# Attention and token mixing on one core: constants ahead of the queries, a gate behind them, masks behind the scores

## The chip, the core and the metric

The kernel runs on one core of a Trainium2 chip. The core has a matrix engine (TensorE, PE in the profile), a vector engine (VectorE, DVE), a scalar engine (ScalarE, ACT), a general engine (GpSimd, POOL) and a queue engine (SyncE, SP) that issues transfers. Each engine works through its own list of instructions in order and waits on semaphores for the others. The metric is the device time of one execution in microseconds, as the median of several.

## The reference

Three stages follow one another; the first feeds `x` into the second, the second into the third.

```python
# 1  attention: B=2, H=8, S=768, D=64; 32-row blocks, window 16
k_sum = k.reshape(B,H,24,32,D).max(3);  v_sum = v.reshape(B,H,24,32,D).mean(3)
scores_l = where(|i-j| < 16, q @ k.T / 8, -1e9)
scores_s = q @ k_sum.T / 8 + log(32)
a = softmax(concat[scores_l, scores_s]);  x = a @ concat[v, v_sum]
# 2  token mixing: x is (2, 768, 512)
theta = x @ w_theta
y = w_tok_r @ (x*cos(theta)) + w_tok_i @ (x*sin(theta));  u = x + y
x = u + relu(u @ w_ch)
# 3  gated unit
h = gelu(x @ w_in);  u, v = halves(h);  v_n = layernorm(v) * g_ln
out = x + (u * (w_sg @ v_n + b_sg)) @ w_out
```

## The kernel before

**Attention.** The sixteen heads form eight pairs p = 0..7 (four for each batch). One pair has four score groups g = 4p + 2hf + h (hf the half of the rows, h the head). A row block of 64 queries sees a window of 96 keys (WK) and the 24 block summaries (NS), 120 columns (WC) in all. For each half the program has these steps, with the tile names that the trace shows:

- prep_k: `ks` is the block maximum of the keys (DVE); `kv<-k` copies the overlapping windows, `kv<-ks` the summaries behind them.
- prep_v: `vsp` (PE) sums the values by block, `vs` copies the sum out, `kv<-vs` spreads it under each window's values.
- scores: two mask matmuls (bf16, identity times `mask`) write `S` and start the accumulation, then 24 score matmuls add to it. `nb` is the row maximum (DVE), `P` the exponentials (ACT), `PT` the transposed `P` (PE), `Pt` its copy, `O` the product with the values (PE), `ri` and `x` the normalisation (DVE), `X` the transposed result (PE), `xT` its copy.

**Token mixing and the gated unit.** `th` (theta) takes 4 × 3 matmuls of 128x512 for each of twelve row tiles, `xs` being its split input: every fp32 product is three fp32r matmuls, hi·hi, hi·lo and lo·hi. Then come `y` with the weights `w_r` and `w_i`, `ch`, `u`, `sg` and `o`. Weights arrive as raw fp32 and are split by shifts on DVE (`cw_...`, three instructions: shift, shift-and-or, shift-and-or) and copies.

**What sets the order.** Nothing is looped in the final program. A list scheduler (`Plan.play`) assigns each step to an engine and writes each engine's list out, from costs in the text of the kernel, from due times shifted by the table BIAS, from a charge STAY for switching kinds of matmul, from weights LOAD by which an engine is chosen where two or three can do a step (one set before its time 80, another behind it), and from the number of buffers of each kind in HOMES. All loads go through SP's one list, in the order of PLAN["want"]; `theta` in PLAN says where the theta tiles start among the score groups. `warm` at the start runs a row of fills (`wps`), matmuls without use for the result.

Of the kernel before, what the change touches and what calls it, by code (L numbers as in the profile page):

```python
# [24 lines left out]
WK = 96  # L25
# [24 lines left out]
class Plan:  # L50
# [257 lines left out]
    def backlog(self, e, c, ready, ready_t, now):  # L308
# [5 lines left out]
SKIP = {}  # L314
ROUNDS = 1
BIAS = {
    "M": 25, "PT": -2, "S": -1, "abs": 4, "ba_": -5, "blocks": 25, "bs_": 8, "bsg": -24,
    "ch___": -2, "cos": 19, "craw": -6, "g": -5, "gf__": -8, "gm__": -5, "gs__h": -1,
    "gs__l": 15, "id": -18, "ident": 4, "k": 1, "ki": 7, "kk": 13, "kw_": -19, "mask": -10,
    "max": 1, "norm_": 1, "o___": -7, "ob__": 12, "q": -14, "q_": -2, "quarter": -9, "ra": 4,  # L320
    "rb": -4, "rc": -11, "rec_": -3, "sg___": -14, "sin": -6, "small": -4, "sq": 2,
    "st__": 26, "th_": -9, "uT__": 13, "u___": -7, "us__h": 2, "us__l": 8, "v_": -17,
    "v__": 7, "vf_": -4, "vnh_": -4, "vnl_": 21, "vs_": 16, "vsc": -7, "vsg": 1, "vsp": 2,
    "w_ch.": 1, "w_ch.h": -9, "w_ch.hi": -7, "w_ch.lo": 13, "w_i.": -3, "w_i.h": 8,
    "w_i.hi": -12, "w_i.lo": 7, "w_inu.": -9, "w_inu.h": 10, "w_inu.hi": 4, "w_inu.lo": 13,
    "w_inv.": -4, "w_inv.h": 1, "w_inv.hi": 4, "w_inv.lo": -10, "w_out.": 6, "w_out.h": 11,
    "w_out.hi": -14, "w_out.lo": -2, "w_r.": -18, "w_r.hi": -1, "w_r.lo": 9, "w_ri.": 5,
    "w_ri.h": -1, "w_ri.hi": 1, "w_ri.lo": -6, "w_sg.": 8, "w_sg.hi": 24, "w_sg.lo": -7,
    "w_sgs.": 1, "w_sgs.hi": -8, "w_sgs.lo": 8, "w_th.": 1, "w_th.h": -4, "w_th.lo": -2,
    "warm": -21, "warm_end": -10, "xT_": -5, "x__": 8, "xh": 2, "xs__h": 3, "xs__l": -13,  # L330
    "y__": 2, "ys_": -14, "z_": 2, "zeros": -13, "zh_": -6, "zl_": -2,
}
TRACE = 0
STAY = 15.5

LOAD = ({"ACT": 0.71, "DVE": 1.34, "POOL": 0.92}, {"ACT": 0.08, "DVE": 1.79, "POOL": 23.66},
        80.0)

PLAN = {
    "want": [("pair", 0), ("pair", 1), ("th", 0), ("pair", 2), ("pair", 3), ("th", 1), ("pair", 4),
             ("th", 3), ("th", 2), ("pair", 5), ("r", 0), ("i", 0), ("pair", 7), ("pair", 6),
             ("i", 1), ("r", 1)],
    "ahead": 0,
    "theta": [20, 26, 27, 28, 29, 36],
    "filler": 20,
    "prep_v": 0,
    "one": 1,
# [5 lines left out]
def kernel(  # L355
# [131 lines left out]
    def load_pair(p):  # L487
        b, r = divmod(p, NP)
        for hf in range(2):
            plan.at(("q", p, hf), f"kv{p}_0")  # L490
        if p:
            load(f"q{p}", lambda: T(f"kv{p}_0")[:, :S], qT[b, r], [("q", p, 0), ("q", p, 1)])
        else:
            load("q0_0", lambda: T("kv0_0")[:, :S // 2], qT[b, r][:, :S // 2], [("q", p, 0)])
            buf("craw", "t")
            load("craw", lambda: T("craw")[:, :P + 3 * WC], consts, ["craw"])
            load("q0_1", lambda: T("kv0_0")[:, S // 2:S], qT[b, r][:, S // 2:], [("q", p, 1)])
        for j, (t, c, w0, w1) in enumerate(vpart[p]):
# [191 lines left out]
    def scores(p, hf):  # L690

        gs = [4 * p + 2 * hf + h for h in range(2)]
        for g in gs:
            buf(f"S{g}", "ps")
            buf(f"P{g}", "t")
            buf(f"nb{g}", "nb")
            for t in range(3):
                plan.at((f"P{g}", t), f"P{g}")

        def masks(e):  # L700
            for g in gs:
                PE.matmul(T(f"S{g}")[:, :3 * WC], id16[:], mask[:, hf * WC:(hf + 3) * WC], start=True,
                          stop=False, skip_group_check=True)

        def mm(e):
            for t in range(3):
                for ab in range(2):
                    for h, g in enumerate(gs):
                        r0 = slice(64 * h, 64 * h + 64)
                        w = 6 * hf + 2 * t + ab  # L710
                        j, kv, c = window(kpart[p], w, WC)
                        PE.matmul(T(f"S{g}")[64 * ab:64 * ab + 64, t * WC:(t + 1) * WC],
                                  T(f"kv{p}_0")[r0, 64 * w:64 * w + 64], T(kv)[r0, c:c + WC],
                                  start=False, stop=True, skip_group_check=True)

        js = (0,) if hf == 0 else (0, 1)
        ss = [f"S{g}" for g in gs]
        op(f"M{gs[0]}", {"PE": 0.32}, masks, ["id16", "mask", *["mask2"] * hf], ss)
        op(f"S{gs[0]}", {"PE": 0.7}, mm,
           [("q", p, hf), *((x, p, j) for j in js for x in ("k", "ks"))], ss, mode="S")  # L720
        for g in gs:
            ps, pt, nb = f"S{g}", f"P{g}", f"nb{g}"
            op(f"max{g}", {"DVE": 0.51}, lambda e, ps=ps, nb=nb: DVE.tensor_reduce(  # L723
                out=T(nb)[:], in_=T(ps)[:, :3 * WC].rearrange("p (t c) -> p t c", c=WC),
                axis=AX.X, op=ALU.max, negate=True), [ps], [nb])
            for t in range(3):
# [398 lines left out]
    def fill(n, z=None):  # L1125

        for j in range(n):
            PE.matmul(T("wps")[:, :4 * WC], id16[:] if z is None else z[:, :P],
                      mask[:] if z is None else z[:, P:P + 4 * WC], start=True, stop=True)
# [8 lines left out]
        T("zeros")[:, :64 + 2 * WC].bitcast(BF16), 0.0), [], ["zeros"])  # L1138
    op("mask", {"DVE": 0.3}, lambda e: DVE.memset(mask[:], 0.0), [], ["mask"])
    op("small", {"POOL": 0.4}, small, [], ["consts"])  # L1140
    op("warm", {"PE": 4.5}, lambda e: fill(12, T("zeros")[:].bitcast(BF16)), ["zeros"], ["wps"])

    def want_th(c):
        weights(("th", c), [rows(w_theta, c)])
# [214 lines left out]
```

## Time and profile before

| | |
|---|---|
| three timed runs | 397.71, 406.56, 403.67 us, median 403.67 |
| the profiled execution's own time | 399.96 us |
| its span in the trace | 398.2 us (1.8 us lie around it) |
| TensorE busy | 388.1 us, 97% of the span, 2899 matmuls |
| VectorE busy | 282.5 us, 71% |
| ScalarE busy | 199.6 us, 50% |
| GpSimd busy | 49.0 us, 12% |
| TensorE's granted clock, mean | 1.0 of full speed |

The shares are means over the whole span, and the attention part fills roughly the first 80 us of it, beside the theta tiles. The page's slices show GpSimd busy in the first ninety microseconds alone, and the transfers at their highest share up to about 55 us.

### The profile page before, as it was taken

To read this page: it belongs to the slowest core of one execution; us is meant where nothing else is said; L and a number is where in the kernel's file an instruction comes from. 1 tells how busy PE (TensorE), PEld (TensorE's weight loads), DVE (VectorE), ACT (ScalarE), POOL (GpSimd) and SP (SyncE) were. 2 spreads that over 40 slices of the span, in tenths; PEclk is the share of its full clock that TensorE was granted. 3 is DMA by queue.
4 is the path that set the end of the run, shared out by engine and by line. 5 is a ranking of instruction groups with operands and counts; after the bars stand their busy time and mean duration, and the time that the engine had idled before them with its cause. 6 is when DMAs were issued, how large, how long until landed. Compare 5 with 4: busy or idle time off the path is not lost.

```text
span 398.2 us, 7273 instructions
## 1 busy us (share of the span) xinstructions
PE 388.1 (97%) x2899; PEld 324.9 (82%) x2899; DVE 282.5 (71%) x542; ACT 199.6 (50%) x415; POOL 49.0 (12%) x81
## 2 busy tenths in 40 slices
PE   7898999999999999999999999999999999999996
PEld 3666667778888888889999988889888889888986
DVE  3769979999999997689999889483454146315442
ACT  3686878668999943244673516274110035411100
POOL 1567886220000000000000000000000000000000
PEclk9999999999999999999999999999999999999999
DMA  8999995310010011338930032010001101000012
GB/s 229 291 282 297 287 252 200 109 54 2 0 34 20 0 54 53 93 96 299 404 130 0 2 106 105 2 53 2 0 0 43 38 28 40 15 0 0 16 44 102
DMA packets 15970, 37.63 MB, mean 95 GB/s; under 512 B 1984, under 2 KB 4928, under 8 KB 15936
## 3 DMA queue, kind: packets, MB, share of 16 engines
q1 hardware_dynamic: 15936, 37.16, 30.0%
q8 instruction: 23, 0.38, 0.4%
q14 instruction: 11, 0.09, 0.1%
HBM read 34.01 MB, written 3.15 MB: 93 GB/s over the span
## 4 chain that ended last, share of the span: by engine, by line
PE 86%; DMA 9%; DVE 3%; SPq 1%; ACT 1%; issue 0%; DVEq 0%
PE y L444 8%; PE y L443 8%; PE y L445 8%; DMA k<-in_kT_dram 4%; PE sg L445 4%; PE sg L444 4%; PE sg L443 4%; PE th L443 3%; PE ch L445 3%; PE ch L443 3%; PE o L445 3%; PE ch L444 3%; PE o L444 3%; PE o L443 3%; PE u L445 3%; PE u L444 3%
## 5 line engine op out<-in xcount | busy, mean ns | idle before, releaser
L431 ACT ACTIVATE g<-gf 128x512 fp32r<-128x512 f32 (+1 forms) x16 | 8.4, 525 | 59.7 <-DVE gf L1100 59.7
L1097 DVE SCALAR_TENSOR_TENSOR gf<-sg,g_sb,bsg 128x512 f32<-128x512 f32 (+1 forms) x16 | 9.9, 617 | 36.4 <-PE sg L445 36.4
L728 ACT ACTIVATE P<-S,nb 128x120 f32<-128x120 f32 x96 | 27.5, 370 | 8.5 <-DVE nb L723 8.1
L444 PE MATMUL y<-w_ri,zs 128*128 128x256 f32 x96 | 27.1, 282 | 0.0
L443 PE MATMUL y<-w_ri,zs 128*128 128x256 f32 x96 | 27.1, 282 | 0.0
L445 PE MATMUL y<-w_ri,zs 128*128 128x256 f32 x96 | 27.0, 282 | 0.0
L443 PE MATMUL ch<-u,w_ch 128*128 128x512 f32 (+1 forms) x64 | 21.7, 338 | 0.0
L445 PE MATMUL ch<-u,w_ch 128*128 128x512 f32 (+1 forms) x64 | 21.6, 338 | 0.0
L444 PE MATMUL o<-g,w_out 128*128 128x512 f32 (+1 forms) x64 | 21.6, 337 | 0.0
L445 PE MATMUL o<-g,w_out 128*128 128x512 f32 (+1 forms) x64 | 21.6, 337 | 0.0
L444 PE MATMUL ch<-u,w_ch 128*128 128x512 f32 (+1 forms) x64 | 21.6, 337 | 0.0
L443 PE MATMUL o<-g,w_out 128*128 128x512 f32 (+1 forms) x64 | 21.6, 337 | 0.0
L444 PE MATMUL u<-x,w_inu 128*128 128x512 f32 (+1 forms) x64 | 21.5, 336 | 0.0
L443 PE MATMUL u<-x,w_inu 128*128 128x512 f32 (+1 forms) x64 | 21.5, 336 | 0.0
L445 PE MATMUL u<-x,w_inu 128*128 128x512 f32 (+1 forms) x64 | 21.5, 336 | 0.0
L443 PE MATMUL th<-w_th,xs 128*128 128x512 f32 x48 | 20.3, 424 | 0.0
L445 PE MATMUL sg<-w_sg,vn 128*128 128x512 f32 x48 | 19.0, 397 | 0.0
L444 PE MATMUL sg<-w_sg,vn 128*128 128x512 f32 x48 | 19.0, 395 | 0.0
L443 PE MATMUL sg<-w_sg,vn 128*128 128x512 f32 x48 | 18.9, 393 | 0.0
L444 PE MATMUL y<-w_i,zs 128*128 128x512 f32 x48 | 18.8, 392 | 0.0
L445 PE MATMUL th<-w_th,xs 128*128 128x512 f32 x48 | 18.8, 392 | 0.0
L444 PE MATMUL y<-w_r,zs 128*128 128x512 f32 x48 | 18.8, 392 | 0.0
(197 smaller groups left out, 1167.3 us busy)
## 6 DMA issues: line engine op xcount, KB each, us to landing
k<-in_kT_dram SPq DMA_DIRECT2D x8, 384.0 KB, 8.1
w_r<-in_w_rT_dram SPq DMA_DIRECT2D x6, 512.0 KB, 6.4
w_i<-in_w_iT_dram SPq DMA_DIRECT2D x6, 512.0 KB, 4.6
kv<-in_vW_dram SPq DMA_DIRECT2D x8, 341.2 KB, 9.3
kv<-in_qT_dram SPq DMA_DIRECT2D x7, 384.0 KB, 9.5
w_th<-in_w_theta_dram SPq DMA_DIRECT2D x4, 512.0 KB, 7.9
w_ch<-in_w_ch_dram SPq DMA_DIRECT2D x4, 512.0 KB, 4.7
w_inv<-in_w_in_dram SPq DMA_DIRECT2D x4, 512.0 KB, 6.2
```

The lines of the kernel that those rows point to most:

```text
L431: e.activation(dst, src, AF.Copy, scale=scale)
L443: PE.matmul(ps, ah, bh, start=first, stop=False, skip_group_check=True)
L444: PE.matmul(ps, ah, bl, start=False, stop=False, skip_group_check=True)
L445: PE.matmul(ps, al, bh, start=False, stop=last, skip_group_check=True)
L728: ACT.activation(T(pt)[:, t * WC:(t + 1) * WC], T(ps)[:, t * WC:(t + 1) * WC], AF.Exp, bias=T(nb)[:, t:t + 1], scale=1.0),
L1097: lambda e: DVE.scalar_tensor_tensor(out=T(gf)[:, :n], in0=T(ps)[:, :n], scalar=g_sb[:, f:f + 1], in1=T("bsg")[:, o:o + n], op0=ALU.mult, ...
```

## The change

- `craw` (the constants: identity and masks) is loaded second, ahead of both halves of pair 0's queries, and behind these stands a transfer of one element, `gate`, that reads `craw`. It can't be issued before `craw` has landed, and every later load stands behind it in SP's list.
- The mask matmuls stand behind the score matmuls and close the accumulation; they cover the 3 × 96 key columns and no longer the summary columns (288 columns instead of 360). The first score matmuls of each column block start it.
- The row of fills at the start has 9 instead of 12.
- The tables are set anew: BIAS, STAY, LOAD, the load order `want`, the theta starts; buffers of kind c (`cw_`) 3 to 2, of kind r 6 to 7.

By the two programs' lists, VectorE has 508 rows instead of 533, ScalarE 368 instead of 362, GpSimd 103 instead of 86, TensorE 2199 instead of 2203. 24 steps go from VectorE to ScalarE (eight `xT` copies, the copies of five `vsc`, three `Pt` among them) and seven to GpSimd; 16 go from ScalarE to GpSimd (copies of windows and spreads); six go from GpSimd to ScalarE, three to VectorE, and five from ScalarE to VectorE.

```diff
-HOMES = {"w": 31, "t": 7, "c": 3, "r": 6, "x": 4, "ps": 8, "ks": 2, "nb": 4, "ri": 3, "st": 3, "mv": 1, "rs": 1}
+HOMES = {"w": 31, "t": 7, "c": 2, "r": 7, "x": 4, "ps": 8, "ks": 2, "nb": 4, "ri": 3, "st": 3, "mv": 1, "rs": 1}
...
-    "M": 25, "PT": -2, "S": -1, "abs": 4, "ba_": -5, "blocks": 25, "bs_": 8, "bsg": -24,
+    "M": 23, "PT": -9, "PV": -3, "Pt": -2, "S": -8, "X_": 1, "abs": 23, "ba_": -2,
...
-STAY = 15.5
+STAY = 13.5
-
-LOAD = ({"ACT": 0.71, "DVE": 1.34, "POOL": 0.92}, {"ACT": 0.08, "DVE": 1.79, "POOL": 23.66},
+LOAD = ({"ACT": 3.5, "DVE": 7.65, "POOL": 0.67}, {"ACT": 1.31, "DVE": 8.05, "POOL": 98.87},
         80.0)
...
-    "want": [("pair", 0), ("pair", 1), ("th", 0), ("pair", 2), ("pair", 3), ("th", 1), ("pair", 4),
-             ("th", 3), ("th", 2), ("pair", 5), ("r", 0), ("i", 0), ("pair", 7), ("pair", 6),
-             ("i", 1), ("r", 1)],
+    "want": [("pair", 0), ("pair", 1), ("th", 0), ("pair", 2), ("th", 2), ("pair", 3), ("pair", 4), ("th", 1), ("pair", 5), ("th", 3), ("i", 0), ("pair", 7), ("r", 1), ("r", 0),
+             ("i", 1), ("pair", 6)],
     "ahead": 0,
-    "theta": [20, 26, 27, 28, 29, 36],
+    "theta": [23, 23, 24, 29, 29, 34],
...
-            load("q0_0", lambda: T("kv0_0")[:, :S // 2], qT[b, r][:, :S // 2], [("q", p, 0)])
             buf("craw", "t")
             load("craw", lambda: T("craw")[:, :P + 3 * WC], consts, ["craw"])
-            load("q0_1", lambda: T("kv0_0")[:, S // 2:S], qT[b, r][:, S // 2:], [("q", p, 1)])
+            for x in range(2):
+                c0 = x * S // 2
+                load(f"q0_{x}", lambda c0=c0: T("kv0_0")[:, c0:c0 + S // 2],
+                     qT[b, r][:, c0:c0 + S // 2], [("q", p, x)])
+
+            op("gate", {"SP": 0.06}, lambda e: e.dma_start(gate[:], T("craw")[0:1, 0:1]),
+               ["craw"], ["gate"], dma=0.01)
...
-        def masks(e):
-            for g in gs:
-                PE.matmul(T(f"S{g}")[:, :3 * WC], id16[:], mask[:, hf * WC:(hf + 3) * WC], start=True,
-                          stop=False, skip_group_check=True)
-
         def mm(e):
...
-                                  start=False, stop=True, skip_group_check=True)
+                                  start=t == 0, stop=False, skip_group_check=True)
+
+        def masks(e):
+            def keys(x):
+                return x.rearrange("p (t c) -> p t c", c=WC)[:, :, :WK]
+
+            for g in gs:
+                PE.matmul(keys(T(f"S{g}")[:, :3 * WC]), id16[:],
+                          keys(mask[:, hf * WC:(hf + 3) * WC]), start=False, stop=True,
+                          skip_group_check=True)
...
-        op(f"M{gs[0]}", {"PE": 0.32}, masks, ["id16", "mask", *["mask2"] * hf], ss)
         op(f"S{gs[0]}", {"PE": 0.7}, mm,
            [("q", p, hf), *((x, p, j) for j in js for x in ("k", "ks"))], ss, mode="S")
+        op(f"M{gs[0]}", {"PE": 0.28}, masks, ["id16", "mask", *["mask2"] * hf], ss)
...
-    op("warm", {"PE": 4.5}, lambda e: fill(12, T("zeros")[:].bitcast(BF16)), ["zeros"], ["wps"])
+    op("warm", {"PE": 3.6}, lambda e: fill(9, T("zeros")[:].bitcast(BF16)), ["zeros"], ["wps"])
```

Three places of the lists. The number behind a tile's name is the program's own count. First the start of SP's list before: keys of pair 0 (`k0`), its queries in halves (`kv0_0`), the constants, its values (`kv0_2`, `kv0_3`, `kv0_0`), the keys of pair 1.

```order
L472 DMA k0_79<-in_kT_dram 128x768
L472 DMA kv0_0_81<-in_qT_dram 128x384
L472 DMA craw_83<-in_consts_dram 128x488
L472 DMA kv0_0_81<-in_qT_dram 128x384
L472 DMA kv0_2_86<-in_vW_dram 96x520
```

The same place now.

```order
L474 DMA k0_81<-in_kT_dram 128x768
L474 DMA craw_83<-in_consts_dram 128x488
L474 DMA kv0_0_85<-in_qT_dram 128x384 x2
L503 DMA gate_72<-craw_83 1x1
L474 DMA kv0_2_106<-in_vW_dram 96x520
```

The constants moved one place forward, and a transfer that waits for them came between the queries and the values. Next, SP's list ahead of pair 6's keys (`k6`), which are the last keys to come; before:

```order
L472 DMA kv5_0_152<-in_vW_dram 96x130
L472 DMA w_r0_327<-in_w_rT_dram 128x512
L472 DMA w_i0_374<-in_w_iT_dram 128x512
L472 DMA k7_398<-in_kT_dram 128x768
L472 DMA kv7_0_400<-in_qT_dram 128x768
L472 DMA kv7_2_473<-in_vW_dram 96x520
L472 DMA kv7_3_483<-in_vW_dram 96x910
L472 DMA kv7_0_400<-in_vW_dram 96x130
L472 DMA k6_577<-in_kT_dram 128x768
```

And now, from the same place:

```order
L474 DMA kv5_0_166<-in_vW_dram 96x130
L474 DMA w_th3_249<-in_w_theta_dram 128x512
L474 DMA w_i0_326<-in_w_iT_dram 128x512
L474 DMA k7_380<-in_kT_dram 128x768
L474 DMA kv7_0_386<-in_qT_dram 128x768
L474 DMA kv7_2_423<-in_vW_dram 96x520
L474 DMA kv7_3_498<-in_vW_dram 96x910
L474 DMA kv7_0_386<-in_vW_dram 96x130
L474 DMA w_r1_508<-in_w_rT_dram 128x512
L474 DMA w_r0_558<-in_w_rT_dram 128x512
L474 DMA w_i1_595<-in_w_iT_dram 128x512
L474 DMA k6_597<-in_kT_dram 128x768
```

`w_r1` and `w_i1` moved ahead of pair 6's keys; the other weights there were ahead of them before too, so it is two more weight blocks. Last, VectorE's list around pair 6's block maximum `ks6` before:

```order
L723 TENSOR_REDUCE nb19_950<-S19_884 128x3
L614 TENSOR_REDUCE ks6_961<-k6_577 128x24
L786 TENSOR_SCALAR ri4_0_987<-O4_0_952 128x6
L789 RECIPROCAL ri4_0_987<-ri4_0_987 128x6
L783 TENSOR_TENSOR x1_0_993<-O4_0_952,ri4_0_987 128x3x128
L723 TENSOR_REDUCE nb20_1001<-S20_946 128x3
```

VectorE's list around `ks6` now:

```order
L795 TENSOR_TENSOR x1_0_1015<-O4_0_936,ri4_0_1009 128x3x128
L440 COPY vs_71<-vsp5_975 24x130
L621 TENSOR_REDUCE ks6_1026<-k6_597 128x24
L548 TENSOR_SCALAR cw_i0_1052<-w_i0_326 128x512
L551 SCALAR_TENSOR_TENSOR cw_i0_1052<-w_i0_326,cw_i0_1052 128x512
L798 TENSOR_SCALAR ri4_1_1092<-O4_1_1059 128x6
L801 RECIPROCAL ri4_1_1092<-ri4_1_1092 128x6
L795 TENSOR_TENSOR x1_1_1097<-O4_1_1059,ri4_1_1092 128x3x128
```

`ks6` stood ahead of the normalisation that feeds `X4_0`, and stands now one half later, with two shifts of `w_i0`'s split, ahead of the one that feeds `X4_1`. On TensorE the same place, which has `X4_0` with theta's first tile behind it, reads before:

```order
L737 MATMUL PT18_995<-ident_66,P18_959 120x128 x3
L795 MATMUL X4_0_1004<-ident_66,x1_0_993 128x128 x3
L443 MATMUL th0_1012<-w_th0_487,xs0_887 128x512
L444 MATMUL th0_1012<-w_th0_487,xs0_887 128x512
L445 MATMUL th0_1012<-w_th0_487,xs0_887 128x512
L443 MATMUL th0_1012<-w_th1_648,xs0_887 128x512
```

TensorE's list around `X4_1` now:

```order
L749 MATMUL PT21_1083<-ident_66,P21_1017 120x128 x3
L445 MATMUL th0_1088<-w_th0_443,xs0_932 128x512
L446 MATMUL th0_1088<-w_th0_443,xs0_932 128x512
L447 MATMUL th0_1088<-w_th0_443,xs0_932 128x512
L445 MATMUL th0_1088<-w_th1_825,xs0_932 128x512
L446 MATMUL th0_1088<-w_th1_825,xs0_932 128x512
L447 MATMUL th0_1088<-w_th1_825,xs0_932 128x512
L807 MATMUL X4_1_1107<-ident_66,x1_1_1097 128x128 x3
L715 MATMUL S24_1117<-kv6_1_1033,kv6_0_657 64x120
```

Before, all twelve matmuls of `th0` stood ahead of `X4_1`; now six of them do, and the other six stand behind it and the scores S24.

## Rows read from the trace of the kernel before

**Rows 1.** The page's part 2, gigabytes a second in 40 equal slices.
```profile
GB/s 229 291 282 297 287 252 200 109 54 2 0 34 20 0 54 53 93 96 299 404 130 0 2 106 105 2 53 2 0 0 43 38 28 40 15 0 0 16 44 102
```

**Rows 2.** What TensorE waited for, first 54 us: total, times, longest.
```profile
PE X L795 <- DVE x L783: 3.8, 5, 0.9
PE S L702 <- DVE mask L438: 0.7, 1, 0.7
```

**Rows 3.** The chain that ended last, 20 to 62 us: start, us, what.
```profile
36.03 1.86 DVE cw_th L541
...
42.20 9.37 DMA k<-in_kT_dram
...
51.66 0.95 DVE ks L614
...
53.56 0.55 PE X L795 x3
54.11 0.23 PE th L443
```

**Rows 4.** SP's timeline, start and us of each issue.
```profile
0.74 0.38 SPq L472 DMA_DIRECT2D k<-in_kT_dram  x1
...
2.58 1.37 SPq L472 DMA_DIRECT2D kv<-in_vW_dram  x3
...
43.06 0.35 SPq L472 DMA_DIRECT2D kv<-in_qT_dram  x1
44.43 3.66 SPq L472 DMA_DIRECT2D kv<-in_vW_dram  x3
```

**Rows 5.** What SP waited for, 42 to 46 us.
```profile
SPq L472 <- DMA w_i<-in_w_iT_dram: 1.0, 1, 1.0
SPq L472 <- DMA w_r<-in_w_rT_dram: 0.4, 1, 0.4
```

**Rows 6.** The timeline of all engines, 0 to 24 us.
```profile
1.49 4.98 PE L1128 MATMUL wps<-zeros 128*128 128x480 bf16 x12 [1.49 <-DVE zeros L1137]
...
3.71 0.95 DVE L614 TENSOR_REDUCE ks<-k 128x24 f32<-128x768 f32 x1 [2.27 <-DMA k<-in_kT_dram]
...
6.59 0.31 ACT L431 ACTIVATE ident<-craw 128x128 f32<-128x128 f32 x1 [1.53 <-DMA craw<-in_consts_dram]
...
7.19 0.77 PE L702 MATMUL S<-mask,id 128*128 128x360 bf16 x4 [0.72 <-DVE mask L438]
...
13.28 0.84 PE L712 MATMUL S<-kv,kv 64*64 64x120 f32 x24
```

**Rows 7.** TensorE's timeline, 48 to 63 us.
```profile
51.13 1.06 PE L712 MATMUL S<-kv,kv 64*64 64x120 f32 x24
...
61.15 0.49 PE L795 MATMUL X<-ident,x 128*128 128x128 f32 x3
61.48 0.47 PE L702 MATMUL S<-mask,id 128*128 128x360 bf16 x2
```

**Rows 8.** DVE's groups by form, first 100 us: count, busy and mean ns.
```profile
L438 DVE COPY xT<-X 128x384 f32<-128x384 f32 x8 | 4.3, 550 | 0.3 <-PE X L795 0.3
...
L438 DVE COPY kv<-vs 24x910 f32<-24x910 f32 x2 | 2.2, 1094 | 0.1
...
L544 DVE SCALAR_TENSOR_TENSOR cw_i<-w_i,cw_i 128x512 int32<-128x512 int32 x3 | 2.0, 682 | 0.0
...
L438 DVE COPY vs<-vsp 24x130 f32<-24x130 f32 x6 | 1.7, 276 | 0.2
...
L541 DVE TENSOR_SCALAR cw_i<-w_i 128x512 int32<-128x512 int32 x3 | 1.3, 425 | 0.0
```

**Rows 9.** POOL's groups by form, first 100 us, one row.
```profile
L433 POOL TENSOR_SCALAR kv<-vs 24x520 f32<-24x520 f32 x7 | 4.3, 620 | 0.5 <-DVE vs L438 0.2
```

**Rows 10.** Busy by stretch: PE, PEld, DVE, ACT, POOL, then granted clock, DMA share, GB/s.
```profile
40.00:50.00 10.00, 9.05 (x153) 6.71 (x153) 9.44 (x24) 8.63 (x26) 8.36 (x13) 1.00 1.04 287
...
100.00:150.00 50.00, 50.00 (x220) 40.94 (x220) 49.25 (x84) 43.55 (x78) 0.00 (x0) 1.00 0.07 22
```

More of the change, by code (lines that the diff above doesn't have):

```diff
@@ L316 @@
 BIAS = {
-    "M": 25, "PT": -2, "S": -1, "abs": 4, "ba_": -5, "blocks": 25, "bs_": 8, "bsg": -24,
[L318 to L328, printed above, removed]
@@ L329 @@
-    "w_sgs.": 1, "w_sgs.hi": -8, "w_sgs.lo": 8, "w_th.": 1, "w_th.h": -4, "w_th.lo": -2,
-    "warm": -21, "warm_end": -10, "xT_": -5, "x__": 8, "xh": 2, "xs__h": 3, "xs__l": -13,
-    "y__": 2, "ys_": -14, "z_": 2, "zeros": -13, "zh_": -6, "zl_": -2,
+    "M": 23, "PT": -9, "PV": -3, "Pt": -2, "S": -8, "X_": 1, "abs": 23, "ba_": -2,
+    "blocks": 6, "bs_": 9, "bsg": -25, "ch___": -8, "cos": 2, "craw": 18, "den_": 14,
+    "exp_": -7, "g": 18, "gate": -8, "gf__": -16, "gs__h": -3, "gs__l": 1, "id": -22,
@@ new lines @@
+    "ident": 23, "k": 13, "ki": -2, "kk": -13, "ksum": -8, "ksw_": -29, "mask": -25, "max": 1,
+    "norm_": -1, "o___": -11, "ob__": 25, "q": -11, "q_": 13, "quarter": -12, "ra": 8,
+    "rb": 7, "rc": -29, "rec_": -8, "sg___": -7, "small": -9, "sq": 7, "st__": 5, "th_": -18,
+    "uT__": -16, "u__": 5, "u___": -8, "us__h": 26, "us__l": 9, "v_": 9, "v__": 3, "vf_": -10,
+    "vnh_": 26, "vnl_": 10, "vs_": 18, "vsc": -24, "vsg": 16, "vsp": 2, "vsq": -12, "vsw_": 5,
+    "w_ch.": -3, "w_ch.h": 9, "w_ch.hi": 1, "w_ch.lo": 10, "w_i.": -17, "w_i.h": 11,
@@ new lines @@
+    "w_i.hi": -24, "w_i.lo": 30, "w_inu.": 12, "w_inu.h": 14, "w_inu.hi": -11,
+    "w_inu.lo": -13, "w_inv.": 4, "w_inv.h": 13, "w_inv.hi": 3, "w_inv.lo": -4, "w_out.": 1,
+    "w_out.h": 9, "w_out.hi": -6, "w_out.lo": 7, "w_r.": 4, "w_r.h": 6, "w_r.hi": -28,
+    "w_r.lo": 22, "w_ri.": -3, "w_ri.h": -15, "w_ri.hi": -17, "w_ri.lo": -1, "w_sg.": -25,
+    "w_sg.hi": 3, "w_sg.lo": 9, "w_sgs.": -14, "w_sgs.hi": -6, "w_sgs.lo": 4, "w_th.": -23,
+    "w_th.h": -21, "w_th.hi": -10, "w_th.lo": 13, "warm": -12, "warm_end": -11, "xT_": 6,
@@ L332 @@
+    "x__": 7, "xh": -16, "xl": 11, "xs__h": 5, "xs__l": -8, "y__": -3, "ys_": -20, "z_": 3,
+    "zeros": -3, "zh_": -3, "zl_": -5,
 }
 TRACE = 0
-STAY = 15.5
-LOAD = ({"ACT": 0.71, "DVE": 1.34, "POOL": 0.92}, {"ACT": 0.08, "DVE": 1.79, "POOL": 23.66},
+STAY = 13.5
+LOAD = ({"ACT": 3.5, "DVE": 7.65, "POOL": 0.67}, {"ACT": 1.31, "DVE": 8.05, "POOL": 98.87},
         80.0)
 PLAN = {
-    "want": [("pair", 0), ("pair", 1), ("th", 0), ("pair", 2), ("pair", 3), ("th", 1), ("pair", 4),
-             ("th", 3), ("th", 2), ("pair", 5), ("r", 0), ("i", 0), ("pair", 7), ("pair", 6),
-             ("i", 1), ("r", 1)],
+    "want": [("pair", 0), ("pair", 1), ("th", 0), ("pair", 2), ("th", 2), ("pair", 3), ("pair", 4), ("th", 1), ("pair", 5), ("th", 3), ("i", 0), ("pair", 7), ("r", 1), ("r", 0),
+             ("i", 1), ("pair", 6)],
@@ L417 @@
     vs_sb = cp.tile([P, VC], F32, tag="vs", name="vs")
+    gate = cp.tile([1, 1], F32, tag="gate", name="gate")
     half_pi = cp.tile([P, 1], F32, tag="hpi", name="half_pi")
```

## The prediction

> **What bounds the kernel now.** I began with TensorE, busy for 388.1 of 398.2 us: all its idle time together is 10.1 us, so a change that leaves its work alone can win no more than that. The view of what TensorE waited for puts the idle time into the first 54 us, and more than half of what it lists into five waits of the transposition X for VectorE's normalisation, 3.8 us together, the longest 0.9 [rows 2]. From there on TensorE never stops: in 100 to 150 us its busy time equals the window [rows 10]. So the end is fixed by two things: when TensorE becomes saturated, and how much work is left to it then. Nothing that the tables do to VectorE or ScalarE behind that point counts, as long as they stay ahead.
>
> Then I read the chain that ended last, backwards from the saturated part [rows 3]. It goes from theta's matmuls at 54.11 to X at 53.56, from there to VectorE's block maximum of pair 6's keys at 51.66, and that maximum waits for a transfer issued at 42.20. The transfers run at 282 to 297 GB/s in slices 3 to 5 [rows 1], as fast as they do anywhere in the first 50 us. SP's issues at 43.06 and 44.43 wait for the landing of w_r and w_i [rows 4, 5], which stand eight places ahead of them in SP's list: only so many loads are in flight, and the list is a line. But VectorE is busy for 9.44 us of 40 to 50 [rows 10]. Loads and VectorE are nearly level, so relief of one alone is soon eaten by the other.
>
> As the mark of saturation I take X of pair 4's second half, X4_1, which starts at 61.15 before [rows 7]: behind it both programs are saturated.
>
> **The start.** The keys of pair 0 are issued at 0.74 [rows 4] and used at 3.71 [rows 6], 2.97 us for 384 KB. At 291 GB/s [rows 1] 1.32 of these are transfer, so 1.65 pass from issue to the first bytes. The constants, 244 KB, come next in the line, 0.84 us more: they land near 4.65. Now they are used at 6.59 [rows 6]. The gate and the values behind it are issued then, three issues taking 1.37, so 0.46 each [rows 4]: the values go out at about 5.1 instead of 2.58, and their bytes flow from 6.75. What was ahead of the gate (keys, constants, queries, 1012 KB) is through at 2.39 + 3.48 = 5.87. **The bubble in the line of loads is 0.9 us.** If the constants share the line with the queries and land at 6.59 as before, it is 2.7; if something fills it, 0. I take 0.9, since the second transfer in line has nothing ahead of it but the keys. Pair 0's scores no longer wait 0.7 for the mask [rows 2]: nine fills end at 1.49 + 9 × 0.415 = 5.2 instead of 6.47 [rows 6] and the scores may begin near 6 instead of 7.19. That is worth nothing at the end, because pair 1's keys come 0.9 later and pair 1 starts with them: 13.28 + 0.9 = 14.2 [rows 6].
>
> **Two weights ahead of pair 6's keys.** In SP's list the keys k6 move behind two more weight blocks of 512 KB. By the page's 287 GB/s [rows 10] that is 1.83 us each, 3.6 together; by the spacing of the issues that wait for a landing (42.20, 43.06, 44.43: 0.86 for w_r, 1.37 for w_i) [rows 3, 4] it is 1.1 each. I take 2.2, the sum of the two, since they follow landings of just such blocks, and keep 1.7 to 3.6. So k6 is there at 51.6 + 0.9 + 2.2 = 54.7.
>
> **VectorE's path from k6 to X4_1.** From the maximum's start to X it took 53.56 − 51.66 = 1.90 [rows 3]. The list puts two shifts of w_i0 between, 0.43 and 0.68 [rows 8]. X4_1 therefore can't start before 54.7 + 3.0 = 57.7, where it started at 61.15. The maximum moved one half later in the list, so the keys may be late without holding that half; that is what pays for the two weights.
>
> **The compute side of the same point.** From pair 1's scores at 13.28 [rows 6] to pair 5's at 51.13 [rows 7] four pairs pass, 9.46 us each. In them VectorE loses three X copies of 0.55, four copies of 0.276 and one spread of 1.09 [rows 8], 3.85 us. If all of it is passed on, pair 5's scores start at 14.2 + 37.85 − 3.85 = 48.2, if none is, at 52.0. From there to X4_1 it took 10.0; the wait of 0.9 at X4_0 goes [rows 2], six of theta's twelve matmuls go at 0.23 each (54.11) [rows 3], 1.4, and a mask pair, a transposition and half a value group come ahead, about 1.1 at the 0.33 between X and the mask behind it [rows 7]. That leaves 8.8: X4_1 between 57.0 and 60.8. As VectorE is busy 94% of the time there [rows 10], most of the relief should pass on, and then the two sides meet. **I take 58.3 for X4_1, 2.85 earlier.**
>
> **What is left behind it.** The six theta matmuls now lie behind X4_1, 1.39 us more. The masks cover 288 columns instead of 360; from the 0.23 of a 512-column matmul [rows 3] 72 columns are 0.03, eight masks lie behind, 0.24. Those ahead of X4_1 are in the cadence. Scores first and masks behind leave the way to the row maximum as long as it was, and cost nothing that a row shows. For c buffers 3 to 2, r 6 to 7, and the twenty-four copies moved to ScalarE in all I book nothing behind saturation: ScalarE is busy 43.55 and VectorE 49.25 of the 50 us in 100 to 150, and TensorE still did not stop [rows 10]. If that cover fails for one stage I would expect a wait like the present ones, 0.9 at most [rows 2].
>
> **Sum.** 399.96 − 2.85 + 1.39 − 0.24 = **398.3 us** against the profiled execution's own 399.96, −1.7; with the bounds of X4_1, 397.0 to 400.8. That execution lies 3.7 below the median 403.67, and the four known executions have a mean of 402.0. Taken from the mean, −1.7 gives **400.3**, which I predict. Some 2% (8 us) is about what a measurement of this kernel can tell from no change, and most of the outcomes lie inside it.
>
> **Rivals.** *Faster.* No bubble, because other transfers cover the gap, and weights at 0.86 each: k6 at 51.6 + 1.7 = 53.3 and X4_1 at 56.3 by VectorE's path. The compute side, 0.9 earlier too, allows 56.1. Then the execution takes 399.96 − 4.85 + 1.15 = 396.3. For it: the 0.86 was taken by a block of this very size. Against: no other load stands ahead of the gate to fill the gap.
>
> *The gate doesn't do what it says.* The constants still come at 6.59 and hold the loads back to 7.05. The bubble is 2.7, k6 lands at 56.5, X4_1 starts at 59.5, the execution takes 399.5. For it: the constants, third in line, are used 2.9 after the keys, where their own 244 KB and the 192 KB of queries ahead of them take 1.5, so transfers in flight do share the line.
>
> *TensorE at the lower clock.* The twelve fills take 0.415 us each for 480 columns [rows 6], which is the 1.2 GHz level; a 512-column matmul takes 0.23 later [rows 3], the 2.4 GHz level, though the granted clock in the profile's rows reads 1.00 throughout. The fills run without a break for 4.98 us before it rose. Now there are nine, 3.7 us, and then a gap near 1 us until the queries and keys are there. If the rise comes only within pair 0 or 1, the work of a pair doubles. A pair takes 9.46, of which no more than that can be TensorE's: at half the clock it takes between 0 more, if its waits for loads and VectorE hide all, and 9.5. I take the middle, 5 us of delay for a pair. One pair gives 403.3, two 408.3, three 413.3; it is slower than before from the first, and measurably so from two on. Against: the loads that pairs 0 and 1 wait for leave room, and scores follow soon after the fills.
>
> The Trainium skill bears on this rival: its page "TensorE: Matmul & The Clock Gate", section "What's actually happening", says that the throttled state is the default and activity releases it. The trace agrees with its first half: the fills run at the lower level from the start. Whether nine are enough no run here shows; by that rule a break behind too few of them is what would hurt.
>
> *GpSimd in VectorE's way.* Net 14 of the steps that change engines come to GpSimd, at 0.62 [rows 9] 8.7 us, about half of it ahead of X4_1. The same shift that takes 0.425 in the mean of w_i [rows 8] held the chain for 1.86 at 36.03 [rows 3], with GpSimd at work. If 4.3 us of new GpSimd work block VectorE in full, X4_1 starts at 62.6 and the execution takes 402.6. Against: most of VectorE's rows show no such stretch.
>
> The Trainium skill states this as a rule: on the page "SBUF — State Buffer", section "Who interferes with whom", the port pair that VectorE and GpSimd share is an exclusive lock, held for a whole instruction. The 1.86 us agree; by it moving copies from VectorE to GpSimd gains less than VectorE's rows say.
>
> **How the numbers follow.** The forecast has a chance of 0.50, the faster rival 0.18, the gate that comes late 0.13, the lower clock 0.12, the blocked VectorE 0.07. From the mean instead of the profiled execution the cases are 400.3, 398.3, 401.5, 405.3 to 415.3, and 404.6. Single executions of one kernel lie 397.71 to 406.56 apart, so a median can be some 3 off either way. The range goes from 394.5 (the faster case, 3.8 below) to 406.0 (the blocked VectorE, and one slow pair). Faster by over 2% means under 395.6, which needs the faster case with luck, or executions that fall together at the lower end: 0.13. Slower by over 2%, over 411.7, needs three pairs at the lower clock or a stage behind 61 us that stops TensorE, and gets 0.07.
>
> **What the changed profile would show.** If right: the values of pair 0 issued near 5.1; a gap under 1 us in the transfers near 6; pair 1's scores near 14.2; k6's maximum near 54.7; X4_1 near 58.3; TensorE without waits behind it; TensorE's busy time down by about 2 us (three fills of 0.415, 32 masks of 0.03). I am wrong if TensorE's waits list y, ch, u or o lines behind 62 us, if 512-column matmuls or scores run at half pace behind 6 us, or if X4_1 starts outside 57.0 to 60.8.

## The result and the profile after

The changed kernel takes 403.12 us as the median of 20 runs (400.35 to 406.68), the kernel before 402.73 in 20 runs (397.71 to 406.56). The ratio of the two is 1.0074, with a 95% interval of 1.0052 to 1.0096. The ratio leaves out executions that lie over 1.5% above the fastest of their own kernel (in run e1 below 16 of 35 of the kernel before and none of the 12 of the changed one), so it compares the faster executions, which reach down to 397.71 us before and to 400.35 now, while over all executions the medians are 0.1% apart. The change is inside 2%, but on the other side of what was forecast: by the ratio about 3 us slower, by the medians level, where 1.7 us faster was expected.

The trace taken with the result is of the slowest of the 20 executions (406.68), in which the transfers ran at 261 to 288 GB/s in slices 2 to 6; before they ran at 282 to 297 in slices 3 to 5 [rows 1]. A second trace of the same kernel (run e1 below: 401.78 the execution, 399.9 its span) has 280 to 305, and it is the one that is read here beside the rows of before. What TensorE waited for in it, total, times, longest:

```profile
PE X L807 <- DVE x L795: 4.3, 2, 3.1
PE wps L1140 <- DVE zeros L1149: 1.2, 1, 1.2
PE vsp L666 <- DMA kv<-in_vW_dram: 1.2, 2, 0.7
PE S L715 <- POOL kv L435: 1.1, 2, 0.8
```

Five waits of X with 0.9 at most [rows 2] have become two, and one of them lasts 3.1 us. The chain that ended last, 34 to 40 us, shows where (start, us, what):

```profile
27.30 8.82 DMA k<-in_kT_dram
...
36.63 0.95 DVE ks L621
...
37.91 0.57 DVE x L795
...
38.62 0.71 PE X L807 x3
```

This is pair 5's block maximum and X2_0, not pair 6's and X4_1 as in [rows 3]. VectorE's and TensorE's timelines of the same trace, first around X2_0, then around X4_1:

```profile
36.63 0.95 DVE L621 TENSOR_REDUCE ks<-k 128x24 f32<-128x768 f32 x1 [3.40 <-DMA k<-in_kT_dram]
...
55.49 0.93 DVE L621 TENSOR_REDUCE ks<-k 128x24 f32<-128x768 f32 x1
56.35 0.94 DVE L548 TENSOR_SCALAR cw_i<-w_i 128x512 int32<-128x512 int32 x1
57.33 1.31 DVE L551 SCALAR_TENSOR_TENSOR cw_i<-w_i,cw_i 128x512 int32<-128x512 int32 x1
```
```profile
12.64 0.85 PE L715 MATMUL S<-kv,kv 64*64 64x120 f32 x24 [0.28 <-POOL kv L435]
...
38.62 0.71 PE L807 MATMUL X<-ident,x 128*128 128x128 f32 x3 [3.09 <-DVE x L795]
39.26 0.96 PE L715 MATMUL S<-kv,kv 64*64 64x120 f32 x24
40.15 0.66 PE L724 MATMUL S<-mask,id 128*128 128x288 bf16 x2
40.61 1.48 PE L749 MATMUL PT<-ident,P 128*120 128x128 f32 x6
42.02 1.48 PE L768 MATMUL O<-kv,Pt 120*64 120x65 f32 x24
43.43 0.85 PE L715 MATMUL S<-kv,kv 64*64 64x120 f32 x24
...
60.22 0.49 PE L807 MATMUL X<-ident,x 128*128 128x128 f32 x3
```

The maximum of 36.63 waited 3.40 us for pair 5's keys; the one of pair 6, at 55.49, waited for nothing. Behind 38.62 no row of TensorE has a wait: it is saturated from X2_0, 15 us earlier than before, where the last wait stood at 53.56. By itself that is worth little, since TensorE's idle time in all is 11.1 us now (399.9 − 388.8) and was 10.1 before. And the groups from 39.26 to 42.02 are drawn out; the windows of the same trace (busy of PE, PEld, DVE, ACT, POOL, then the granted clock, DMA share, GB/s) say why:

```profile
36.00:38.00 2.00, 0.00 (x0) 0.00 (x0) 1.30 (x4) 0.12 (x1) 1.80 (x5) 1.00 1.08 242
38.00:40.00 2.00, 1.38 (x27) 0.96 (x27) 1.97 (x3) 0.64 (x3) 1.53 (x2) 0.96 0.99 270
40.00:42.00 2.00, 2.00 (x14) 1.43 (x8) 1.04 (x3) 0.67 (x3) 1.81 (x3) 0.50 1.03 401
42.00:44.00 2.00, 2.00 (x46) 1.91 (x48) 0.38 (x3) 1.87 (x7) 0.00 (x0) 0.68 1.07 278
44.00:46.00 2.00, 1.95 (x45) 1.28 (x37) 2.00 (x4) 0.89 (x4) 0.71 (x2) 1.00 1.06 206
```

TensorE did nothing in 36 to 38, and then the granted clock reads 0.50, the 1.2 GHz level, in 40 to 42 and 0.68 in 42 to 44. What the gate did is seen in SP's timeline (start and us of each issue):

```profile
1.18 0.42 SPq L474 DMA_DIRECT2D craw<-in_consts_dram  x1
1.64 0.91 SPq L474 DMA_DIRECT2D kv<-in_qT_dram  x2
4.44 0.71 SPq L503 DMA_DIRECT2D gate<-craw  x1
5.20 1.29 SPq L474 DMA_DIRECT2D kv<-in_vW_dram  x3
```

The constants were there at 4.4 and the values went out at 5.20, where 4.65 and 5.1 were forecast. Between them the transfers all but stand: 8 GB/s in 5 to 6 us, 334 in the same stretch of e2, which leaves the gate out.

### The profile page after: what moved, and what is told of

The parts are those of the page before. It is cut to its first block, busy times and chain, and to the rows that moved or that the text cites. A ratio compares the mean times of both kernels' runs of the same rounds, so it can differ in the third digit from the quotient of the medians.

```text
span 404.8 us, 7304 instructions
## 1 busy us (share of the span) xinstructions
PE 392.3 (97%) x2897; PEld 326.8 (81%) x2897; DVE 272.1 (67%) x517; ACT 196.7 (49%) x423; POOL 58.9 (15%) x98
## 4 chain that ended last, share of the span: by engine, by line
PE 83%; DMA 14%; SPq 1%; DVE 1%; issue 0%
PE y L446 8%; PE y L445 8%; PE y L447 8%; DMA k<-in_kT_dram 8%; PE sg L445 4%; PE sg L447 4%; PE sg L446 4%; PE th L445 3%; PE o L445 3%; PE o L447 3%; PE o L446 3%; PE u L445 3%; PE v L445 3%; PE ch L445 3%; PE ch L446 3%; PE u L447 3%
## 5 line engine op out<-in xcount | busy, mean ns | idle before, releaser
L1130 DVE TENSOR_TENSOR ob<-o,xT 128x512 f32<-128x512 f32 (+1 forms) x16 | 8.8, 556 | 22.0 <-PE o L447 22.0
L735 DVE TENSOR_REDUCE nb<-S 128x3 f32<-128x360 f32 x32 | 15.5, 526 | 11.4 <-PE S L724 11.2
L445 PE MATMUL sg<-w_sg,vn 128*128 128x512 f32 x48 | 19.0, 396 | 0.0
L445 PE MATMUL v<-w_inv,x 128*128 128x512 f32 x48 | 18.9, 395 | 0.0
L446 PE MATMUL v<-w_inv,x 128*128 128x512 f32 x48 | 18.9, 394 | 0.0
## 6 DMA issues: line engine op xcount, KB each, us to landing
kv<-in_qT_dram SPq DMA_DIRECT2D x7, 384.0 KB, 11.1
```

What stands on the lines that cost most here:

```text
L445: PE.matmul(ps, ah, bh, start=first, stop=False, skip_group_check=True)
L446: PE.matmul(ps, ah, bl, start=False, stop=False, skip_group_check=True)
L1130: op(f"ob{b}_{half}_{c}", {"DVE": 0.15 + 0.53 * n / 512}, lambda e: DVE.tensor_tensor(out=T(ob)[:, :n], in0=T(ps)[:, :n], in1=xT[:, c, b * ...
```

## The experiments

All ran beside the kernel before. The medians are over all executions of a run, the ratios are formed as above. The median of the kernel before was 403.29 us beside e1 to e4, 402.56 beside e5 to e8 and 402.52 beside e9 to e11.

| run | edit | median, us | ratio to before, 95% |
|---|---|---|---|
| e1 | the changed kernel again | 402.90 | 1.0066 (1.0018 to 1.0114) |
| e2 | no gate | 401.66 | 0.9995 (0.9953 to 1.0036) |
| e3 | pair 6's keys ahead of w_r1 | 405.98 | 1.0089 (1.0032 to 1.0146) |
| e4 | fills ahead of X1_0, X2_0 | 402.87 | 1.0029 (0.9982 to 1.0076) |
| e5 | ks5 later | 402.66 | 0.9991 (0.9953 to 1.0028) |
| e6 | no gate, ks5 and pair 6's maximum later | 401.62 | 0.9969 (0.9926 to 1.0011) |
| e7 | before, masks behind | 402.45 | 1.0002 (0.9953 to 1.0051) |
| e8 | before, ks5 earlier | 403.72 | 1.0064 (1.0019 to 1.0109) |
| e9 | no gate, ks5 later | 400.71 | 0.9982 (0.9944 to 1.0019) |
| e10 | as e9, maxima of pairs 3 and 4 later | 400.89 | 0.9984 (0.9946 to 1.0022) |
| e11 | before, ks5 earlier, fills ahead of X2_0 | 403.48 | 1.0009 (0.9964 to 1.0053) |

The edits work on the finished lists: a few lines behind `plan.run()` move single instructions or put matmuls in, so every other instruction keeps its place.

**e1, the changed kernel again.** No edit.

> The changed kernel once more, nothing edited, for a second trace and its clock in every execution. In the first trace (404.8 us span, 406.68 the execution) pair 6's keys came at 61.4 and X4_1 at 65.1, where 54.7 and 58.3 were forecast. Theory A, the line of loads is late because of what the change does (gate, more weights ahead of pair 6): the same again, keys at 60 to 62, X4_1 at 64 to 66 in any execution. Theory B, that execution's transfers were slow by chance: from a span near 401 and the 339.7 that followed X4_1, X4_1 near 61.3 and the keys near 57.5. Theory C, TensorE's clock: stretches at the lower level behind the long waits at 29.8 and 43.2, and a mean clock of 0.992 to 0.996 in every execution, where the kernel before shows 1.0.

X4_1 started at 60.22 and pair 6's maximum at 55.49, without a wait. So theory A in its first form, loads late by the change, is not what holds an execution whose transfers run as before, and the 65.1 of the first trace came with slow transfers. From X4_1 to the end both traces have the same 339.7 (404.8 − 65.1, 399.9 − 60.2). The clock was below 1.0 in 11 of 12 executions here. But it was below 1.0 in 27 of 35 executions of the kernel before too; the one on which I had built had 1.0, as the other eight.

**e2, no gate.**

```diff
-            op("gate", {"SP": 0.06}, lambda e: e.dma_start(gate[:], T("craw")[0:1, 0:1]),
+            op("gate", {"SP": 0.06}, lambda e: None,
```

> The changed kernel without the one-element transfer; every other instruction in its place. If the gate's bubble costs what I forecast (0.9 us in the line of loads, passed on in full), this is 0.5 to 1 us faster than the changed kernel. If the gate is what makes the change lose (theory A in its form gate), 2 to 3 us faster, level with the kernel before. If the constants, now in line with the values, come later and delay pair 0 alone, no difference, since pair 1 waits for its own keys.

The median falls by 1.2 us, between the first two expectations. In the traces, pair 1's maximum starts at 9.90 instead of 10.61 and pair 1's scores at 12.06 instead of 12.64; at X2_0 only 0.25 of that is left:

```profile
38.37 0.85 PE L807 MATMUL X<-ident,x 128*128 128x128 f32 x3 [2.76 <-DVE x L795]
```

The long wait is there without the gate as well, so the gate is not the cause of that wait. How much it costs is not settled: 1.2 us in the medians, from 12 executions each that spread over 5 to 6 us, and 0.3 between the spans of the two traces (399.9 and 399.6); the intervals of the two ratios overlap.

**e3, pair 6's keys earlier.** `k6` and `w_r1` change places in SP's list, and their buffers with them.

```diff
     done = plan.run()
+    swap("w_r1.0", "k6")
```

> The changed kernel with pair 6's keys and w_r1 exchanged in SP's list: the keys now stand ahead of w_r1, w_r0 and w_i1; all engines' lists are as they were. If the keys of pair 6 set the saturation point, they land three weight blocks earlier (3.3 to 5.5 us) and X4_1 moves by the wait that it had for them, 1.3 us in the first trace, no more, since VectorE is then held by pair 7's keys and its own work: 1 to 1.5 us faster. If the weights cost as much as I forecast and nothing else holds X4_1, 2 to 4 us faster. If the earlier pairs' keys set the point (waits of 2.2 and 2.9 at X1_0 and X2_0), under 0.5.

No gain of any size: the median is 3.1 us higher, the ratio not separable from e1's. Its trace (a long execution, 409.2 us of span) shows where an earlier keys' load leads; the waits are of GpSimd and VectorE in 40 to 72 us, of TensorE in all:

```profile
POOL w_r L561 <- DMA w_r<-in_w_rT_dram: 5.0, 1, 5.0
```
```profile
DVE cw_i L548 <- POOL w_i L561: 3.6, 1, 3.6
```
```profile
PE X L807 <- DVE x L795: 9.7, 4, 3.2
```

GpSimd rescales w_r1 before w_i0 in its list, VectorE's shifts of w_i0 stand ahead of the normalisation for X4_1, and so in this trace the late weight stopped TensorE by way of two engines (X4_1 waited 3.22 us, to 67.93): other lists had been built on its coming early. What the weights cost where the change put them, this run can't say.

**e4, the clock held.**

```diff
+        if o.name in ("X1_0", "X2_0"):
+            fill(10)
         o.fn(ENG[o.on])
```

> The changed kernel with ten fills of 480 columns ahead of X1_0 and of X2_0, the two transpositions that waited 2.2 and 2.9 us: TensorE is then busy through the wait. Theory C (the clock falls behind these waits, and the stretches at the lower level are paid): the granted clock stays at 1.0 from 25 to 50 us, and the execution is 1 to 2 us shorter. If the stretches at the lower level lie beside waits for keys anyway: clock 1.0, and the time the same within 0.5. If the fills themselves come in the way (2 us each where the wait is shorter than that): up to 1 us longer.

The clock was 1.0 through 25 to 50 us of the trace and 0.999 or 1.0 in 8 of 12 executions (1 of 12 in e1). The median did not move, and the ratio, 1.0029, lies between e1's and 1 with an interval that covers both. Not settled by this run.

**e5, ks5 later.**

```diff
     done = plan.run()
+    behind("norm2_0", "ksum5")
```

> The changed kernel with one VectorE instruction moved: the block maximum of pair 5's keys (ks5) stands behind the normalisation that feeds X2_0, not ahead of it; nothing else. In the second trace of the changed kernel VectorE waited 3.4 us there for the keys, X2_0 3.1 us for VectorE, from 35.9 before to 38.6, TensorE's clock fell for 3.5 us behind it, and TensorE never waited again to the end. Theory D (this place in VectorE's list is the new bound): X2_0 at 36 to 36.5, the stretch at the lower clock gone, and the execution 1.5 to 3 us shorter than the changed kernel, at most until pair 6's keys (54.7) stop X4_1. Theory A (the loads as such): the wait moves to the next consumer of the keys, the scores of pair 5 or pair 6's maximum, and the time stays within 0.7.

The ratio goes from 1.0066 to 0.9991 (the intervals just overlap); the median over all only from 402.90 to 402.66. The first of these is 0.4 below the kernel before beside it, the second 0.1 above, so the medians show no gain. The clock was 1.0 in 6 of 12 executions, against 1 of 12 in e1. The trace (397.7 span, transfers at 296 to 324 GB/s) shows the mechanism. TensorE's timeline, the same list as in e1:

```profile
35.48 0.60 PE L807 MATMUL X<-ident,x 128*128 128x128 f32 x3
36.01 0.84 PE L715 MATMUL S<-kv,kv 64*64 64x120 f32 x24
...
38.65 0.85 PE L715 MATMUL S<-kv,kv 64*64 64x120 f32 x24
...
41.43 0.92 PE L768 MATMUL O<-kv,Pt 120*64 120x65 f32 x24 [1.02 <-POOL kv L435]
...
48.78 0.57 PE L768 MATMUL O<-kv,Pt 120*64 120x65 f32 x12 [1.37 <-POOL kv L435]
...
57.96 0.55 PE L807 MATMUL X<-ident,x 128*128 128x128 f32 x3
```

X2_0 comes 3.1 us earlier; up to 35 us the two traces lie within 0.1 us of each other. From X2_0 to the next scores but one TensorE needs 3.17 us (38.65 − 35.48) where it needed 4.81 in e1 (43.43 − 38.62) for the same instructions: the lower clock cost 1.64 us. Of the 4.8 us so won, 2.4 are lost again in two waits of value groups for copies on GpSimd, and X4_1 is 2.26 us earlier than in e1, the span 2.2.

**e6, three things undone.**

```diff
+    behind("norm2_0", "ksum5")
+    behind("norm4_1", "ksum6", "ksw6_1", "ksw6_0")
+    behind("max23", "w_i0.0", "w_i0.1")
```

and the gate left out as in e2.

> The changed kernel with three things undone: no gate, ks5 behind the normalisation of X2_0, and pair 6's maximum with its copies and the two shifts of w_i0 behind the normalisations of X4_1. By theory D with the measured price of the gate (1.2 to 1.6 us): 3 to 5 us shorter than the changed kernel, so 398 to 400 as a median and 2.5 to 4 below the kernel before. If the loads hold the end whatever the order is: as without the gate alone, 401.7.

X4_1 came at 56.98, but the scores behind it stopped in their last group:

```profile
59.21 0.42 PE L715 MATMUL S<-kv,kv 64*64 64x120 f32 x3 [0.97 <-issue]
```

The trace names no cause of this wait, but ScalarE's last copy of pair 6's summaries, one of the steps moved, ran just then:

```profile
59.01 0.32 ACT L433 ACTIVATE kv<-ks 128x96 f32<-128x96 f32 x1
```

That points to what was moved behind X4_1 being late for S24 instead. The median, 401.62, is that without the gate alone, and not the 398 to 400 of theory D.

**e7, masks alone.** The kernel before with the mask function and the accumulation flags of the change, and each mask pair moved behind its scores.

```diff
+    for p in range(B * NP):
+        for g in (4 * p, 4 * p + 2):
+            behind(f"S{g}", f"M{g}")
```

> The kernel before with one part of the change: the two mask matmuls behind the 24 of the scores, on 288 columns; all else in the order of before. By my forecast 32 x 0.03 us less work on TensorE, of which that ahead of saturation (24 of them) is hidden: 0.2 to 1.0 us shorter, not separable from no change. If the masks at the end lengthen the way from the scores to the row maximum: up to 0.3 for each half ahead of the saturation point, 2 to 3 us longer.

1.0002: nothing lost, nothing that can be told from no change. In its trace 336.6 us follow X4_1 (404.7 − 68.07), 0.4 less than the 337.05 of the kernel before (398.2 − 61.15).

**e8, the one instruction in the kernel before.**

```diff
     done = plan.run()
+    i, j = (next(i for i, o in enumerate(done) if o.name == n) for n in ("den2_0", "ksum5"))
+    done.insert(i, done.pop(j))
```

> The kernel before with the one VectorE instruction put where the change put it: ks5 ahead of the normalisation that feeds X2_0, nothing else. Theory D: X2_0 waits for the keys that land at 37.65, so it goes from 35.9 to about 39.6, TensorE's clock falls behind the wait, and the execution is 2 to 4 us longer than before, as much as the changed kernel or more. Theory A, or if the late keys of pair 6 (51.6) hide all of it: the same within 0.7.

The ratio is 1.0064, where the whole change had 1.0066 in e1, and the median is 1.2 us above that of the kernel before beside it. Its trace has the new wait, and behind it the lower clock (VectorE's and TensorE's timeline, then two windows; the transfers were slower in this execution, 261 to 278 GB/s in slices 2 to 5, and X2_0 came at 42.59 where 39.6 was expected):

```profile
40.69 0.95 DVE L614 TENSOR_REDUCE ks<-k 128x24 f32<-128x768 f32 x1 [3.65 <-DMA k<-in_kT_dram]
```
```profile
42.59 0.90 PE L795 MATMUL X<-ident,x 128*128 128x128 f32 x3 [4.19 <-DVE x L783]
```
```profile
42.00:44.00 2.00, 1.41 (x6) 1.14 (x6) 1.97 (x4) 0.36 (x1) 0.00 (x0) 0.61 1.04 272
44.00:46.00 2.00, 2.00 (x19) 0.95 (x20) 0.31 (x2) 1.75 (x5) 0.75 (x2) 0.53 1.01 364
```

**e9, no gate and ks5 later.** The edits of e2 and e5.

> The changed kernel without the gate and with ks5 behind the normalisation of X2_0, pair 6's maximum left where the change put it. If the two prices add (gate 1.2 in the median, ks5 2.2 between the two traces taken at the same transfer rate): 399.5 to 401 in the median, and 0.990 to 0.996 of the kernel before in undisturbed runs. If both feed the same wait and only the larger counts: as ks5 alone, 0.997 to 1.001. A first matmul group of S24 that stops TensorE, as with pair 6's maximum moved, must not show here, since that stays in its place.

400.71, 2.2 us under the changed kernel's median in e1 and 1.8 under that of the kernel before in the same session (402.52). The median lies where the first expectation put it, the ratio, 0.9982, where the second did. So it isn't settled whether the two prices add, and as the ratio can't be told from 1, the kernel isn't shown to beat the kernel before.

**e10, pairs 3 and 4 as well.**

```diff
+    behind("norm1_0", "ksum3", "ksw3_0")
+    behind("norm1_1", "ksum4", "ksw4_1")
```

> As the kernel without gate and with ks5 later, and in addition the block maxima of pairs 3 and 4 behind the normalisations that feed X1_0 and X1_1. In the first trace of the changed kernel (transfers at 261 to 288 GB/s) these maxima waited 2.5 and 1.7 us for keys and X1_0 2.2 us for VectorE. Theory D for all pairs (a load's consumer ahead of a normalisation stops TensorE whenever the transfers are slow): the executions at the slow transfer rate gain 1 to 2 us, so the upper quartile falls, the fast ones nothing. If the row maxima of the later scores now wait in their place, 0 to 1 us longer.

400.89, nothing more. In its trace the maximum of pair 5's keys waits again, and the value groups and X behind it:

```profile
36.54 0.95 DVE L621 TENSOR_REDUCE ks<-k 128x24 f32<-128x768 f32 x1 [2.22 <-DMA k<-in_kT_dram]
```

**e11, the kernel before with ks5 early and fills.** As e8, and ahead of X2_0:

```diff
+        if o.name == "X2_0":
+            fill(14)
```

> The kernel before with ks5 ahead of the normalisation of X2_0 and fourteen fills of 480 columns (2.9 us at the upper clock) ahead of X2_0, so that TensorE is busy through most of the 4.2 us that it waited there. Theory C as the second half of the price (the wait itself, then the stretch at the lower clock behind it): the granted clock stays at 1.0 there and 1 to 1.7 us come back against ks5 early without fills (403.7 median, 1.0064). If the wait alone is the price: the same as without fills, within 0.5.

The clock stayed at 1.0 behind the wait (all windows from 36 to 48 us). 403.48 against 403.72 in the median, 1.0009 against 1.0064 in the ratio: the medians fit the wait alone, the ratios the clock as part of the price, and the intervals overlap. What the clock takes is better read from the same instructions in e1 and e5.

## Why the prediction was wrong

**The step that failed** is in the compute side: "most of the relief should pass on, and then the two sides meet", with pair 6's keys as the place where they meet. I had read VectorE's list around pair 6's maximum, found it one half later, and never looked at pair 5's. There the maximum had moved one half earlier, from the normalisation for X2_1 to the one for X2_0. In the trace of the kernel before it comes behind the normalisation for X2_0 and waits for nothing, and neither does X2_0 (VectorE, then TensorE):

```profile
35.03 0.56 DVE L783 TENSOR_TENSOR x<-O,ri 128x384 f32<-128x384 f32 x1
39.16 0.93 DVE L614 TENSOR_REDUCE ks<-k 128x24 f32<-128x768 f32 x1
```
```profile
35.89 0.49 PE L795 MATMUL X<-ident,x 128*128 128x128 f32 x3
```

In its new place it comes before the keys (idle 3.40 us), X2_0 waited 3.1, and the clock took 1.64 more. The place alone is enough: in e8, without the change's relief of VectorE, the maximum waited 3.65. e5 undoes this one place and has X4_1 at 57.96; e8 puts it into the kernel before and loses 0.64% in the ratio, 1.2 us in the median. X4_1, forecast for 58.3, stands at 60.22, inside the 57.0 to 60.8 that I gave it, but 0.93 earlier than before instead of 2.85.

That e5's 57.96 lies so near the 58.3 is in part luck. Pair 6's keys landed 1.5 us sooner there than forecast (44.09 + 9.1 = 53.2), the two shifts took 1.55 and 1.31 instead of 0.43 and 0.68, and TensorE had the two waits for GpSimd, 2.4 together, that stand in no term of the forecast.

**What is left behind the point** was mis-sized. Forecast +1.15 (six theta matmuls 1.39, masks −0.24), measured 339.68 − 337.05 = +2.63 (span less start of X4_1, e1 and before). It goes with the list and not with the execution: the first trace, e1, e2, e4, e5, e9 and e10 all have 339.7 us from X4_1 to the end, the traces of before, e8 and e11 337.1. Six theta matmuls are 1.4 of it. The other 1.2 is not explained by any wait: none is listed behind X4_1, and the matmuls are the same but for these six. Measured from each start to the next, theta's take 1.88 us longer in e1's trace than in that of before, the 144 of v 0.56 and the 144 of O 0.30, while those of ch and sg take 0.29 and 0.20 less. So it lies in the pace at which matmuls follow one another, which I had taken as unchanged. Whether their order sets it or the work of other engines beside them, no run tests.

So e1's trace is 1.70 us longer than that of before (399.9 − 398.2 = 2.63 − 0.93) where 1.70 less was forecast, and of these 3.40 us 1.92 lie at X4_1 and 1.48 behind it. With the second, even e5's earlier point is worth only 0.5 us in the span (398.2 to 397.7).

**The gate** was right in its mechanism, a stop in the line of loads. Its size is open: 0.9 forecast, 1.2 in the medians of e2 and e1, 0.3 in the spans of their traces. Pair 1's scores were not held to 14.2; they came at 12.64, 0.6 earlier than before, since its keys were used at 10.61 (before at 10.92).

**Two weights ahead of pair 6's keys** held the keys as forecast and cost nothing in e1: the transfer issued at 44.21 landed 10.5 us later, at the 54.7 of the forecast, and the maximum ran at 55.49 without a wait. With the slow transfers of the first trace it did wait, 1.31 us, so there they may cost something. One figure of that term was misread: 0.86 is no time between two landings, as the issue at 42.20 had last waited for ScalarE (0.2 us), not for a load. Slips in the sum of the start change its bubbles by less than 0.2 us: 3.71 + 0.84 is 4.55 and not 4.65, kilobytes are 1000 bytes there and 1024 in the sum of the weights, and the late gate's bubble comes to 2.8 by its own figures, not 2.7.

**The shifts of w_i0** took 0.94 and 1.31 instead of the 0.43 and 0.68 of [rows 8]. GpSimd was at work beside them:

```profile
56.02 0.99 POOL L435 TENSOR_SCALAR kv<-k 128x672 f32<-128x672 f32 x2
57.09 1.01 POOL L435 TENSOR_SCALAR kv<-vs 24x910 f32<-24x910 f32 x1
```

So the rival of the blocked VectorE was there in kind, and cost nothing here: the normalisation ended at 59.54, and TensorE had work up to X4_1 at 60.22. By the Trainium skill's page "SBUF — State Buffer", section "Who interferes with whom", this pair of engines shares a pair of ports that one of them holds for a whole instruction; the longer shifts agree with that. So does e2, where the second shift went first (56.74) and took 0.69, and GpSimd's copy of 24x910 behind it took 1.33 instead of 1.01.

**The rival of the lower clock** came true in another place than I had put it: behind the wait at X2_0, not at the start. The Trainium skill's page "TensorE: Matmul & The Clock Gate", section "What's actually happening", calls the throttled state the default that activity lifts; the 0.50 behind an idle TensorE agrees. I had weighed it for the first fills alone and not for each wait that the change could make longer.

**The masks** were right: no change in the time (e7), and 0.4 us less behind X4_1 where 0.24 was forecast. **TensorE's busy time** was forecast to fall by 2 us and rose by 0.7 (388.1 to 388.8). In e5, at a clock of 1.0, it fell by 0.8 (387.3): 1.5 of the miss go with the lower clock, and the other 1.2 is as much as stays unexplained behind X4_1. **The base** was 0.7 too low: I had taken the mean of four executions, 402.0, as enough, where the median of 20 is 402.73.

## What to carry to other kernels

When a change reorders an in-order engine, list every instruction on it that waits for a load, and for each see which instruction behind it TensorE needs; one block maximum, one half too early, held TensorE for 3.1 us, and put into the kernel before it cost 0.64% in the ratio. If TensorE's wait is that long, the stretch at the lower clock is paid on top (1.64 us here), so price each such wait with that stretch. Don't take the stretch behind the last wait as unchanged because no wait stands in it: here the same matmuls took 1.2 us more without one. And look at several executions before choosing the one whose trace is the base.

## What the runs showed that I had not expected

After a wait of 3.09 us TensorE's granted clock was 0.50 in 40 to 42 us, and the same instructions took 4.81 us instead of 3.17; after one of 4.19 us (e8) it was 0.61 and 0.53 in the two windows from 42 to 46; behind waits of 0.9 to 1.4 us (e5, and [rows 2]) it stayed at 1.0. And executions of one kernel differ in how fast their transfers run: the two traces of the changed kernel moved 262 and 301 GB/s in slice 3, pair 6's maximum stood at 61.41 and 55.49, and the spans were 404.8 and 399.9. What sets the rate of an execution stays open.
